# Order of the eight half rows at the seam between the spectral block and the feed-forward block

## The chip, the cores and the metric

The kernel runs on one NeuronCore of a Trainium2 chip, as one program. The metric is the device time of one execution in microseconds (us). Three executions of the kernel before took 1441.19, 1441.78 and 1444.77 us; the median, 1441.78 us, is the time that the changed kernel is compared with.

## What is computed

The input is one sequence of 4096 tokens with 640 channels. A conditioning vector gives six vectors of 640 values: shift, scale and gate for each of two blocks.

```python
h = _layernorm(x) * (1 + ca) + sa
x = x + ga * _A_ref(h, ...)      # 2-D real FFT, block-diagonal complex MLP with soft shrinkage, inverse FFT
h = _layernorm(x) * (1 + cb) + sb
x = x + gb * _B_ref(h, ...)      # (silu(h @ w_gate) * (h @ w_up)) @ w_down, inner width 1728
```

The two blocks are called the spectral block and the feed-forward block here. Everything is float32; matrix products are mostly done with numbers that are split in a high and a low part.

## The kernel before

**Tiling.** The 4096 tokens are seen as a grid of 128 (on the partitions) by 32 (n2). A "row" is one value of n2: 128 tokens by 640 channels. The spectral block goes through its frequencies in eight chunks, `ch` = 0 to 7, of four blocks each, so through 32 slots, p = 4·ch + b. A slot's last steps shrink the values (`shrink`), split them in two (`shrink_high` on ScalarE, `shrink_low` on VectorE: L847, `xl<-xx,xh`), and take the inverse transform over one axis (`stage_i`, L858 to L861: `pi`, then `co`). The result is stored to `s2` in DRAM. The feed-forward block needs rows of the finished inverse transform: a row loads its 128 frequencies from `s2`, multiplies them by a 128 by 128 matrix, gates the product with `gab`, adds the row of x, and normalizes it.

**The seam.** For the first four rows (tile 0 of the feed-forward block) this last part is written out by hand, and this is where the change lies. Each of these rows i = 0 to 3 is made in two halves: `hf` = 0 is the lower 320 columns, `hf` = 1 the upper 320. `cf` (tiles `cfrm` for rows 0 and 1, `cfrr` for rows 2 and 3) holds the frequencies loaded from `s2`. The last of these, 16 of 128, are stored and loaded again late, and for the lower columns only (`inverse_last(i, 0)`: L908 `pi<-tt,bx`, L909 `cz<-pi`, L910 store, then the load in L915). So there are two kinds of half row on TensorE:

- a lower half (L1086) is one product with the whole of `cf`, and waits for the late load;
- an upper half (L1089, L1091) takes the last chunk straight from `tt` in SBUF, four products with `et`, and one more with the first 112 rows of `cf`. It doesn't wait for the late load, and is five products where the lower half is one.

In the trace a product of two float32 operands counts as two matmuls.

**What follows each half row.** `first_y`: VectorE multiplies the sum in PSUM by `gab` (L1095, into one of four 320-column buffers in `acc` and `cl`); GpSimd adds it to x2 (L1096), VectorE for the last two half rows. `first_stats`: VectorE takes the statistics of the half (L1101); at the second half of a row it joins them (L1104, L1105), and GpSimd makes the scale and the shift from them in three small steps (L1106 power -0.5, L1108, L1109). `first_norm`: ScalarE normalizes rows 0, 1 and 2 into `xn` (L1115); row 3 is normalized by VectorE later (L2470). The loop that calls these goes through a list, `order`, of half rows in the order written by hand.

**What stands behind.** `inverse_last(i, 1)` does for the upper columns of the last chunk what was done for the lower ones: `pi` for i = 0 to 3 on TensorE (L908), into two PSUM banks taken in turn, `cz` on ScalarE (L909), and stores that GpSimd issues (L910). So the products of i = 2 and 3 wait until ScalarE has emptied the banks of i = 0 and 1. Then the feed-forward block begins: twenty transposes of `xn` on TensorE (L1923, `pt`, row by row and five to a row), the modulated result and its split (`ht`, `hx`: L1925, L1928, L1930, L1931), and the first gate products (`pg`, L1937 to L1939). The fifth transpose of each row goes to a bank that `inverse_last(3, 1)` has used.

**What sets the order.** Both parts stand under a manual schedule: each engine runs its instructions in an order fixed when the kernel is built, and waits for other engines by semaphores. In the feed-forward block a planner with a table of costs writes the order; it starts behind the seam and is not touched.

Of the kernel before, what the change touches and what calls it, by code (L numbers as in the profile page):

```python
# [9 lines left out]
OP = mybir.AluOpType  # L10
# [161 lines left out]
def body(tc, x, w1, b1, w2, b2, wg, wu, wd, c, wm, k_fa, k_tb, k_tx, k_bm, k_bx, k_ga, k_ge, k_id, out, dbg=None):  # L172
    nc = tc.nc
    pe, act, dve, pool = nc.tensor, nc.scalar, nc.vector, nc.gpsimd
# [27 lines left out]
    with ExitStack() as top:  # L202
# [34 lines left out]
        with ExitStack() as af:  # L237
# [351 lines left out]
            NP = 4 * NCH  # L589
# [274 lines left out]
            on = lambda f, p, *a: f(p // 4, p % 4, *a) if 0 <= p < NP else None  # L864
# [33 lines left out]
            def inverse_last(i, hf):  # L898
                e = slice(320 * hf, 320 * hf + 320)
                J = 4 * ORDER[NCH - 1] + i  # L900
                q, k = i // 2, slice(64 * (i % 2), 64 * (i % 2) + 64)
                if hf == 0:
                    xxs[NCH - 1, i] = p2.tile([P, D], F32, tag="xx", bufs=5, name=f"cz{i}")
                co = xxs[NCH - 1, i]
                pi = (ps.tile([P, 512], F32, tag="p3", name=f"pi{J}_{hf}") if hf == 0 else
                      bank0(i, [P, 512], f"pi{J}_{hf}"))
                for r in range(2):
                    mm(pi[:, :320], bx[k, r, :], tts[NCH - 1, q][k, r, e], start=(r == 0), stop=(r == 1))  # L908
                act.activation(co[:, e], pi[:, :320], AF.Copy)  # L909
                (pool if hf else nc.scalar).dma_start(s2[4 * J:4 * J + 4, :, e].rearrange("k n d -> (k n) d"), co[:, e])  # L910
# [109 lines left out]
            def first_gate():  # L1020
                src = wg.rearrange("(k p) f -> p k f", p=P)
                wraw.append(hp.tile([P, 4, 256], F32, tag="rz", bufs=2, name="wr4"))
                wraw.append(p2.tile([P, 256], F32, tag="wm", bufs=1, name="wr1"))
                nc.sync.dma_start(wraw[0], src[:, 0:4, 0:256])
                nc.sync.dma_start(wraw[1], src[:, 4, 0:256])

            def first_gate_high():
                for k in range(5):
                    act.activation(wh[k], wraw[0][:, k] if k < 4 else wraw[1], AF.Copy)
# [5 lines left out]
            def load_first():  # L1035
                x2 = fx.tile([P, 4, D], F32, tag="gx", bufs=2, name="x2_0")
                nc.sync.dma_start(x2, xv[:, 0:4, :])
                x2s[0] = x2
# [5 lines left out]
            for p in range(LAST + 1, NP):  # L1044
                if p > LAST + 1:
                    on(shrink, p - 5)
                on(stage_l1, p)
                on(tail_l1, p)
                if p == LAST + 1:
                    on(shrink, p - 5)  # L1050
                elif p == LAST + 2:
                    load_first()
                    first_gate()
                for f, *a in sums.get(p, ()):
                    f(*a)
                on(shrink_high, p - 5)
                on(stage_l2, p - 1)
                on(stage_i, p - 6)
                on(shrink_low, p - 5)
            first_gate_high()  # L1060
            on(shrink, LAST - 1)
            on(shrink_high, LAST - 1)
# [13 lines left out]
            x2 = x2s[0]  # L1076
            sts = lp.tile([P, 4, 2, 6], F32, tag="st", bufs=3, name="sts")

            def first_y(i, hf):
                e = slice(320 * hf, 320 * hf + 320)  # L1080
                g0 = et[:, i, 512:640]
                c = cf[i // 2][:, i % 2, e]
                tag = (("b0", "b1", "p1", "p1"), ("p2", "p2", "p3", "p3"))[hf][i]
                py = ps.tile([P, 512], F32, tag=tag, bufs=1 if tag[0] == "b" else 2, name=f"py0_{i}_{hf}")
                if hf == 0:
                    mm(py[:, :320], g0, c, start=True, stop=True)  # L1086
                else:
                    for k in range(4):
                        mm(py[:, :320], et[:, i, 128 * k:128 * k + 128], tts[NCH - 1, k // 2][:, k % 2, e],  # L1089
                           start=(k == 0), stop=False)  # L1090
                    mm(py[:, :320], g0[0:rl], c[0:rl], start=False, stop=True)  # L1091
                n = len(ys)
                y = (acc, cl)[n // 2 % 2][:, 320 * (n % 2):320 * (n % 2) + 320]
                ys.append(y)
                dve.tensor_tensor(y, py[:, :320], gab[:, e], op=OP.mult)  # L1095
                (pool if n < 6 else dve).tensor_tensor(x2[:, i, e], x2[:, i, e], y, op=OP.add)  # L1096


            def first_stats(i, hf):
                e = slice(320 * hf, 320 * hf + 320)  # L1100
                dve.bn_stats(sts[:, i, hf, :], x2[:, i, e])  # L1101
                if hf == i // 2:
                    mv, rs, nm = b1m[:, :, i], ca1[:, i:i + 1], sa4[:, i:i + 1]
                    dve.bn_aggr(mv, sts[:, i])  # L1104
                    dve.tensor_scalar(rs, mv[:, 1:2], EPS, None, op0=OP.add)  # L1105
                    pool.tensor_tensor(rs, rs, mhalf[:, :1], op=OP.pow)  # L1106
                    if i < 3:
                        pool.tensor_tensor(nm, mv[:, 0:1], rs, op=OP.mult)  # L1108
                        pool.tensor_tensor(nm, nm, mone[:, :1], op=OP.mult)  # L1109
                    fst.append((mv, rs, nm))  # L1110

            def first_norm(i):
                mv, rs, nm = fst[i]
                xn = p2.tile([P, D], F32, tag="co" if i < 2 else "wm", bufs=2 if i < 2 else 1, name=f"xn0_{i}")
                act.activation(xn, x2[:, i, :], AF.Identity, bias=nm, scale=rs)  # L1115
                xns[0].append(xn)

            ys = []
            fst = []
            order = [(0, 1), (1, 1), (0, 0), (1, 0), (2, 0), (3, 0), (2, 1), (3, 1)]  # L1120
            for n, (i, hf) in enumerate(order):
                first_y(i, hf)

                for q in ([n - 1] if 0 < n < 6 else [5, 6] if n == 6 else [7] if n == 7 else []):
                    first_stats(*order[q])
                if n in (3, 4):
                    first_norm(n - 3)
            for i in range(4):
                if i == 2:
                    first_norm(2)  # L1130
                inverse_last(i, 1)

        if dbg == "afno":
# [1428 lines left out]
```

## Time and profile before

| | |
|---|---|
| median of three executions | 1441.78 us |
| the profiled execution, its own time | 1442.52 us |
| its span, first to last instruction | 1440.7 us |
| TensorE busy | 1405.0 us, 98% |
| VectorE, ScalarE, GpSimd busy | 76%, 54%, 37% |
| stretch 280.00 to 321.07 us: TensorE busy | 35.98 of 41.07 us |
| the same: VectorE, ScalarE, GpSimd | 28.69, 19.76, 17.19 us |

The seam lies at about 285 to 321 us of the span. In the rows of the profile, PE is TensorE, PEld its weight loads, DVE VectorE, ACT ScalarE, POOL GpSimd and SP the engine that issues most transfers. A row of the timeline has the start, the duration (of several instructions, from the first start to the last end), the engine and line, what is written and read, and the count; in square brackets the time that the engine sat idle before it, and who ended that.

### The profile page before, as it was taken

The numbers are of one execution on the slowest core, as the hardware profiler recorded it, in microseconds if no ns is written. First come the engines' busy times: TensorE is split into PE (matmuls) and PEld (weight loads), VectorE is DVE, ScalarE is ACT, GpSimd is POOL, SyncE is SP. The second block draws the span as 40 slices with busy tenths as digits, with TensorE's granted clock in tenths as the row PEclk, the third lists the DMA queues.
The fourth block names the chain that finished last, engine by engine and source line by source line (L and its number), as shares of the span: only waits on it lengthen the run. The fifth ranks groups of instructions, "written<-read, shape, count | busy, mean of one in ns | idle before, by whom it ended". The sixth has DMA issues, their size and how long they took to land.

```text
span 1440.7 us, 23922 instructions
## 1 busy us (share of the span) xinstructions
PE 1405.0 (98%) x8516; PEld 1329.6 (92%) x8516; DVE 1100.3 (76%) x1979; ACT 783.8 (54%) x1560; POOL 538.6 (37%) x640
## 2 busy tenths in 40 slices
PE   7899999989999999999999999999999999999999
PEld 2699999968889888899999999999999999999998
DVE  8878888868888687767878778788647757567775
ACT  6868877745544545545465556555435345245432
POOL 5300222144444444333244334434324545146533
PEclk9999999999999999999999999999999999999999
DMA  9988798757777989897787997788896666966652
GB/s 375 319 267 261 238 293 257 226 175 248 251 243 256 349 267 303 309 359 259 252 306 237 344 370 242 252 275 284 291 330 225 209 219 237 361 218 226 207 184 91
DMA packets 187383, 382.28 MB, mean 265 GB/s; under 512 B 22240, under 2 KB 104736, under 8 KB 185472
## 3 DMA queue, kind: packets, MB, share of 16 engines
q1 hardware_dynamic: 179072, 364.37, 73.7%
q0 software_dynamic: 6608, 13.77, 3.0%
q10 hardware_dynamic: 1584, 2.62, 0.5%
q8 instruction: 67, 1.10, 0.3%
q14 instruction: 52, 0.43, 0.1%
HBM read 266.66 MB, written 104.86 MB: 258 GB/s over the span
## 4 chain that ended last, share of the span: by engine, by line
PE 80%; DVE 8%; DMA 5%; ACT 3%; issue 2%; SPq 1%; POOL 1%; DVEq 0%; ACTq 0%; POOLq 0%
PE pd L2432 15%; PE pw L2113 8%; PE pw L2115 8%; PE pw L2114 8%; PE pd_X L2294 5%; PE pg L1978 3%; PE pg L1977 3%; PE pg L1979 3%; PE pc L800 3%; PE pl L732 3%; PE pd_Y L2294 3%; PE pw L2124 2%; PE pw L2126 2%; PE pw L2125 2%; PE py L1699 1%
## 5 line engine op out<-in xcount | busy, mean ns | idle before, releaser
L2432 PE MATMUL pd<-wdh,a 128*128 128x320 f32 x1040 | 240.1, 311 | 1.1 <-DVE x L2404 1.1
L2432 PEld LDWEIGHTS pd<-wdh,a 128*128 128x128 f32 x1040 | 177.2, 189 | 1.7 <-DVE x L2404 1.4
L2432 PE MATMUL pd<-wdl,a 128*128 128x320 f32 x540 | 166.7, 310 | 0.0
L1454 DVE TENSOR_TENSOR wb<-r,wb 128x512 fp32r<-128x512 f32 (+3 forms) x154 | 154.7, 1015 | 12.1 <-ACT wb L1451 10.5
L2113 PE MATMUL pw<-h,wt 128*128 128x384 f32 x416 | 141.2, 340 | 2.2 <-ACT s_x L2132 2.2
L2115 PE MATMUL pw<-h,wt 128*128 128x384 f32 x416 | 140.3, 337 | 0.0
L2114 PE MATMUL pw<-h,wt 128*128 128x384 f32 x416 | 139.9, 336 | 0.0
L2404 DVE TENSOR_TENSOR x<-x,pd 128x320 f32<-128x320 f32 x240 | 109.8, 479 | 37.9 <-PE pd L2432 33.6
L1451 ACT ACTIVATE wb<-r 128x512 fp32r<-128x512 f32 (+3 forms) x170 | 117.4, 704 | 35.5 <-PE pw L2126 24.5
L2113 PE MATMUL pw<-h,wb 128*128 128x384 f32 x312 | 105.0, 336 | 0.9 <-DVE x L2404 0.9
L2114 PE MATMUL pw<-h,wb 128*128 128x384 f32 x312 | 104.6, 335 | 0.0
L2115 PE MATMUL pw<-h,wb 128*128 128x384 f32 x312 | 104.6, 335 | 0.0
L1977 PE MATMUL pg<-ht,wb 128*128 128x512 f32 x260 | 102.3, 393 | 0.0
L2432 PEld LDWEIGHTS pd<-wdl,a 128*128 128x128 f32 x540 | 101.9, 189 | 0.3
L1979 PE MATMUL pg<-ht,wb 128*128 128x512 f32 x260 | 101.4, 390 | 0.2 <-DVE wb L1454 0.2
L1978 PE MATMUL pg<-ht,wb 128*128 128x512 f32 x260 | 101.5, 390 | 0.0
L2132 ACT ACTIVATE s_x<-pw 128x384 f32<-128x384 f32 x52 | 25.5, 490 | 121.3 <-PE pw L2115 120.2
L1682 POOL TENSOR_TENSOR cr<-cr,gab 128x640 f32<-128x640 f32 x28 | 46.7, 1670 | 94.1 <-DMA cr<-s 75.9
L2113 PEld LDWEIGHTS pw<-h,wt 128*128 128x128 f32 x416 | 78.1, 188 | 3.8 <-ACT s_x L2132 3.8
L862 POOL DMA_DIRECT2D s<-co x28 | 15.9, 569 | 167.3 <-ACT co L861 158.4
L2114 PEld LDWEIGHTS pw<-h,wt 128*128 128x128 f32 x416 | 78.2, 188 | 0.0
L2115 PEld LDWEIGHTS pw<-h,wt 128*128 128x128 f32 x416 | 78.1, 188 | 0.0
(360 smaller groups left out, 4060.2 us busy)
## 6 DMA issues: line engine op xcount, KB each, us to landing
wt<-td SPq DMA_DIRECT2D x104, 512.0 KB, 5.1
hs<-ho SPq DMA_DIRECT2D x52, 512.0 KB, 5.4
h<-hs SPq DMA_DIRECT2D x32, 768.0 KB, 8.4
r<-in_B_w_up_dram SPq DMA_DIRECT2D x36, 640.0 KB, 5.0
r<-in_B_w_gate_dram SPq DMA_DIRECT2D x36, 640.0 KB, 4.8
wdr<-wdd SPq DMA_DIRECT2D x25, 640.0 KB, 5.9
td<-wt SPq DMA_DIRECT2D x25, 512.0 KB, 5.8
g<-s SPq DMA_DIRECT2D x7, 1280.0 KB, 8.7
```

Of the source, the lines that this page charges most:

```text
L1451: act.activation(wbs[t, n][:, 0, ks, e], raw[t, n][:, ks, e], AF.Copy)
L1454: (pool if onp else dve).tensor_tensor(wbs[t, n][:, 1, ks, e], raw[t, n][:, ks, e], f32(wbs[t, n][:, 0, ks, e]), op=OP.subtract)
L1682: pool.tensor_tensor(crs[r], crs[r], gab, op=OP.mult)
L1977: mm(b, wh, hh, start=(kk == 0), stop=False)
L1978: mm(b, wh, hl, start=False, stop=False)
L1979: mm(b, wl, hh, start=False, stop=(kk == 4))
L2113: mm(b, w(0, kp), a[:, kp, 0], start=start and kp == 0, stop=False, skip_group_check=not start)
L2114: mm(b, w(0, kp), a[:, kp, 1], start=False, stop=False, skip_group_check=not start)
L2115: mm(b, w(1, kp), a[:, kp, 0], start=False, stop=kp == 1, skip_group_check=not start)
L2294: mm(bk[b, i][:, :320], x, y, start=new and j == 0, stop=j == len(seq) - 1, skip_group_check=not new)
L2404: dve.tensor_tensor(x2[:, e], x2[:, e], x[0][:, :320], op=OP.add)
L2432: mm(pd[g, hf][0][:, :320], l, m, start=i == 0, stop=i == len(s) - 1 and not (last and len(gs) > 1))
```

## The change

Three edits, all at the seam:

1. In the last slot (p = 31) `shrink_low` of slot 26 stands ahead of `stage_l2` and `stage_i` instead of behind them, so VectorE makes `xl` ahead of the two additions to `tt`.
2. The half rows come in the order upper 0, 1, 2, then lower 0, 1, 2, then upper 3, lower 3 (before: upper 0, 1, lower 0, 1, 2, 3, upper 2, 3). All rows are complete with their lower half. GpSimd adds seven of the eight half rows instead of six.
3. The three calls of `first_norm` follow half rows 4, 5 and 6 of the list, so all stand ahead of `inverse_last(i, 1)`; before, the third stood between i = 1 and i = 2 of it.

```diff
                 on(shrink_high, p - 5)
+                if p == NP - 1:
+                    on(shrink_low, p - 5)
                 on(stage_l2, p - 1)
                 on(stage_i, p - 6)
-                on(shrink_low, p - 5)
+                if p < NP - 1:
+                    on(shrink_low, p - 5)
...
-                (pool if n < 6 else dve).tensor_tensor(x2[:, i, e], x2[:, i, e], y, op=OP.add)
+                (pool if n < 7 else dve).tensor_tensor(x2[:, i, e], x2[:, i, e], y, op=OP.add)
...
-                if hf == i // 2:
+                if hf == 0:
...
-            order = [(0, 1), (1, 1), (0, 0), (1, 0), (2, 0), (3, 0), (2, 1), (3, 1)]
+            order = [(0, 1), (1, 1), (2, 1), (0, 0), (1, 0), (2, 0), (3, 1), (3, 0)]
             for n, (i, hf) in enumerate(order):
                 first_y(i, hf)
 
-                for q in ([n - 1] if 0 < n < 6 else [5, 6] if n == 6 else [7] if n == 7 else []):
+                for q in ([n - 1] if 0 < n < 7 else [6, 7] if n else []):
                     first_stats(*order[q])
-                if n in (3, 4):
-                    first_norm(n - 3)
+                if n in (4, 5, 6):
+                    first_norm(n - 4)
             for i in range(4):
-                if i == 2:
-                    first_norm(2)
                 inverse_last(i, 1)
```

On TensorE, the half rows of the seam; `py_i_hf` is the PSUM sum of row i, half hf. Before:

```order
L1091 MATMUL py_1_1_3899<-cfrm,et 128x320
L1086 MATMUL py_0_0_3908<-cfrm,et 128x320
L1086 MATMUL py_1_0_3913<-cfrm,et 128x320
L1086 MATMUL py_2_0_3925<-cfrr,et 128x320
L1086 MATMUL py_3_0_3937<-cfrr,et 128x320
L1089 MATMUL py_2_1_3942<-tt_0_3595,et 128x320 x2
L1089 MATMUL py_2_1_3942<-tt_1_3606,et 128x320 x2
L1091 MATMUL py_2_1_3942<-cfrr,et 128x320
L1089 MATMUL py_3_1_3957<-tt_0_3595,et 128x320 x2
L1089 MATMUL py_3_1_3957<-tt_1_3606,et 128x320 x2
L1091 MATMUL py_3_1_3957<-cfrr,et 128x320
L908 MATMUL pi_1_3969<-tt_0_3595,bx 128x320 x2
```

The same place on TensorE with the change (the line numbers are those of the changed file, three higher):

```order
L1094 MATMUL py_1_1_3899<-cfrm,et 128x320
L1092 MATMUL py_2_1_3908<-tt_0_3595,et 128x320 x2
L1092 MATMUL py_2_1_3908<-tt_1_3606,et 128x320 x2
L1094 MATMUL py_2_1_3908<-cfrr,et 128x320
L1089 MATMUL py_0_0_3917<-cfrm,et 128x320
L1089 MATMUL py_1_0_3922<-cfrm,et 128x320
L1089 MATMUL py_2_0_3934<-cfrr,et 128x320
L1092 MATMUL py_3_1_3946<-tt_0_3595,et 128x320 x2
L1092 MATMUL py_3_1_3946<-tt_1_3606,et 128x320 x2
L1094 MATMUL py_3_1_3946<-cfrr,et 128x320
L1089 MATMUL py_3_0_3962<-cfrr,et 128x320
L908 MATMUL pi_1_3971<-tt_0_3595,bx 128x320 x2
```

The upper half of row 2 has moved ahead of the first lower half, and the lower half of row 3 to the end; the number of products is the same.

On ScalarE, from the normalization of row 0 to the first `ht`; `xn_i` are the normalized rows, the four `cz` the evacuations of `inverse_last(i, 1)`, i = 0 to 3 in this order. Before:

```order
L1115 ACTIVATE xn_0_3923<-x_0_3673,sa_72,ca_71 128x640
L1115 ACTIVATE xn_1_3935<-x_0_3673,sa_72,ca_71 128x640
L909 ACTIVATE cz_3859<-pi_1_3969 128x320
L909 ACTIVATE cz_3865<-pi_1_3974 128x320
L1115 ACTIVATE xn_2_3979<-x_0_3673,sa_72,ca_71 128x640
L909 ACTIVATE cz_3871<-pi_1_3981 128x320
L909 ACTIVATE cz_3877<-pi_1_3986 128x320
L1925 ACTIVATE ht_3_4009<-pt_0_4035,sb_74,cb_73 128x512
```

The same place on ScalarE with the change:

```order
L1118 ACTIVATE xn_0_3932<-x_0_3673,sa_72,ca_71 128x640
L1118 ACTIVATE xn_1_3944<-x_0_3673,sa_72,ca_71 128x640
L1118 ACTIVATE xn_2_3960<-x_0_3673,sa_72,ca_71 128x640
L909 ACTIVATE cz_3859<-pi_1_3971 128x320
L909 ACTIVATE cz_3865<-pi_1_3976 128x320
L909 ACTIVATE cz_3871<-pi_1_3981 128x320
L909 ACTIVATE cz_3877<-pi_1_3986 128x320
L1926 ACTIVATE ht_3_4009<-pt_0_4035,sb_74,cb_73 128x512
```

The normalization of row 2 has moved ahead of the first two `cz`.

On GpSimd, from the fifth addition to x2 to the first store of `cz`; `ca` and `sa` are the scale and the shift of a row, in three steps to a row. With the change:

```order
L1099 TENSOR_TENSOR x_0_3673<-x_0_3673,acc 128x320
L1109 TENSOR_TENSOR ca_71<-ca_71,mhalf 128x1
L1111 TENSOR_TENSOR sa_72<-b1m,ca_71 128x1
L1112 TENSOR_TENSOR sa_72<-sa_72,mone 128x1
L1099 TENSOR_TENSOR x_0_3673<-x_0_3673,acc 128x320
L1109 TENSOR_TENSOR ca_71<-ca_71,mhalf 128x1
L1111 TENSOR_TENSOR sa_72<-b1m,ca_71 128x1
L1112 TENSOR_TENSOR sa_72<-sa_72,mone 128x1
L1099 TENSOR_TENSOR x_0_3673<-x_0_3673,cl 128x320
L1109 TENSOR_TENSOR ca_71<-ca_71,mhalf 128x1
L1111 TENSOR_TENSOR sa_72<-b1m,ca_71 128x1
L1112 TENSOR_TENSOR sa_72<-sa_72,mone 128x1
```

Ahead of the three steps of row 2 stand seven additions and the steps of rows 0 and 1; before, there were six additions and the same steps, with one addition fewer ahead of each of the three.

Two more moves need no rows. On TensorE the first two transposes of row 0 stand ahead of the last two `pi` of `inverse_last(i, 1)`; before, all twenty stood behind them. On VectorE the first edit is one move: L847 `xl_2<-xx_2,xh_2` now stands directly behind L774 and ahead of the two L802 `tt<-pc,b2t`, where before it stood behind both.

## Prediction

> **What bounds the kernel now.** First the busy time by stretch. The columns behind the bounds are the length and then the busy us (and count) of PE, PEld, DVE, ACT and POOL.
>
> ```profile
> 280.00:321.07 41.07, 35.98 (x183) 26.70 (x181) 28.69 (x61) 19.76 (x41) 17.19 (x29) 1.00 0.47 153
> 321.07:1440.70 1119.63, 1108.05 (x6554) 1070.12 (x6554) 840.26 (x1449) 548.09 (x1086) 458.16 (x495) 1.00 0.77 265
> ```
>
> Behind the seam TensorE is busy for 1108.05 of 1119.63 us. What remains open there is 11.6 us, and the largest entry of its waits is on another engine's work, not on a transfer:
>
> ```profile
> PE pw L2124 <- ACT s_z L2132: 2.5, 2, 1.9
> ```
>
> Such a wait moves with the work before it. So I carry a shift of the seam's end to the end of the program one to one. Ahead of that, the 41.07 us of the seam have 5.1 us in which TensorE does nothing, and there order can matter. I read the seam on each engine in order of time. First PE:
>
> ```profile
> 298.67 2.32 PE L1089 MATMUL py<-tt,et 128*128 128x320 f32 x8
> 300.82 0.70 PE L1091 MATMUL py<-cfrm,et 112*128 112x320 f32 x2
> 303.27 1.34 PE L1086 MATMUL py<-cfrm,et 128*128 128x320 f32 x4 [1.74 <-DMA cfrm<-s]
> 305.53 2.32 PE L1089 MATMUL py<-tt,et 128*128 128x320 f32 x8
> 307.68 0.70 PE L1091 MATMUL py<-cfrr,et 112*128 112x320 f32 x2
> 310.38 0.70 PE L1091 MATMUL py<-cfrr,et 112*128 112x320 f32 x2
> 311.01 1.35 PE L908 MATMUL pi<-tt,bx 64*128 64x320 f32 x8
> 312.88 1.67 PE L908 MATMUL pi<-tt,bx 64*128 64x320 f32 x8 [0.51 <-ACT cz L909]
> 314.48 2.56 PE L1923 MATMUL pt<-idn,xn 128*128 128x128 f32 x20
> ```
>
> TensorE stands still for 1.74 us until the late load lands (303.27), then runs through to 312.36, waits 0.51 us for `cz`, and makes the transposes. Eight products of an upper half take 307.68 - 305.53 = 2.15 us, so 0.27 each: 2.69 us an upper half, 0.54 a lower half. Now ACT:
>
> ```profile
> 307.74 0.92 ACT L1115 ACTIVATE xn<-x,sa,ca 128x640 f32<-128x640 f32 x1 [11.44 <-POOL sa L1109]
> 312.39 0.77 ACT L909 ACTIVATE cz<-pi 128x320 f32<-128x320 f32 x2 [1.86 <-PE pi L908]
> 313.32 0.92 ACT L1115 ACTIVATE xn<-x,sa,ca 128x640 f32<-128x640 f32 x1 [0.17 <-POOL sa L1109]
> 314.25 0.77 ACT L909 ACTIVATE cz<-pi 128x320 f32<-128x320 f32 x2
> 316.64 0.78 ACT L1925 ACTIVATE ht<-pt,sb,cb 128x512 fp32r<-128x512 f32 x1 [1.62 <-PE pt L1923]
> ```
>
> The first `cz` begins at 312.39, as soon as TensorE delivers. From there everything to the first `ht` (316.64) follows: `pi` of i = 2 and 3 at +0.49, the bank for the fifth transpose free at +2.63 (314.25 + 0.77), `ht` at +4.25. **The seam's end is the first `cz` plus 4.25 us**, as long as `xn` of rows 2 and 3 is there.
>
> **The order of the half rows.** The upper half of row 2 needs nothing late, so it fills the wait. The half row at 298.67 and its L1091 at 300.82 end their issue at 301.36, and row 2's upper half runs from 301.36 to 304.06, past the landing at 303.27. Then three lower halves to 305.68, row 3 upper to 308.38, row 3 lower to 308.92. Before, L1091 at 310.38 issued until 310.92. So TensorE finishes the half rows **2.0 us earlier**, and `pi` of i = 0 and 1 end at 310.36 instead of 312.36. This alone would bring `cz` to 310.39.
>
> **But `cz` no longer waits for TensorE.** On ScalarE it now stands behind `xn` of row 2, and that needs the statistics of row 2, so the additions and the three steps on GpSimd. Their prices, DVE first, then POOL:
>
> ```profile
> 301.57 0.49 DVE L1095 TENSOR_TENSOR acc<-py,gab 128x320 f32<-128x320 f32 x1 [2.20 <-PE py L1091]
> 304.52 0.48 DVE L1101 BATCH_NORM_STATS2 sts<-x 128x6 f32<-128x320 f32 x1
> 304.92 0.47 DVE L1095 TENSOR_TENSOR cl<-py,gab 128x320 f32<-128x320 f32 x1
> 305.58 0.50 DVE L1101 BATCH_NORM_STATS2 sts<-x 128x6 f32<-128x320 f32 x1 [0.18 <-POOL x L1096]
> 306.11 0.21 DVE L1104 BATCH_NORM_AGGREGATE b1m<-sts 128x2 f32<-128x12 f32 x1
> 306.36 0.15 DVE L1105 TENSOR_SCALAR ca<-b1m 128x1 f32<-128x1 f32 x1
> 306.43 0.48 DVE L1095 TENSOR_TENSOR acc<-py,gab 128x320 f32<-128x320 f32 x1
> 306.82 0.48 DVE L1101 BATCH_NORM_STATS2 sts<-x 128x6 f32<-128x320 f32 x1
> ```
>
> ```profile
> 304.68 1.68 POOL L1096 TENSOR_TENSOR x<-x,cl 128x320 f32<-128x320 f32 x2 [1.69 <-DVE cl L1095]
> 306.59 0.58 POOL L1106 TENSOR_TENSOR ca<-ca,mhalf 128x1 f32<-128x1 f32 x1 [0.22 <-DVE ca L1105]
> 307.65 0.87 POOL L1096 TENSOR_TENSOR x<-x,acc 128x320 f32<-128x320 f32 x1
> ```
>
> An addition takes 0.84 us in a pair and 0.86 otherwise. The three steps take 307.65 - 306.59 = 1.06 us until the next addition, and ScalarE's `xn` starts 307.74 - 306.59 = 1.15 after the first of them. VectorE starts 0.05 after a sum is complete (301.52 to 301.57), GpSimd 0.08 after VectorE. From statistics to the end of L1105 is 306.51 - 305.58 = 0.93, to GpSimd 1.01.
>
> So with the change: row 2's upper sum is complete at 304.22, L1095 at 304.27, its addition 304.84 to 305.68. VectorE then waits for that addition with the statistics (305.74), makes L1095 of row 1 lower 0.40 later (306.14, done 306.61), whose addition, the fifth, runs 306.69 to 307.55. Meanwhile the fourth (305.68 to 306.52) completes row 0: statistics at 306.58, L1105 done and handed over at 307.59. From here GpSimd alone sets the pace: three steps 1.06, sixth addition 0.86, three steps 1.06, seventh addition 0.86, that is 3.84 us to 311.43, and then 1.15: `xn` of row 2 at 312.58 (before: 313.32). It holds ScalarE for 0.93 (313.32 to 314.25), so **the first `cz` begins at 313.51 instead of 312.39: +1.1 us**. The two transposes now ahead of `pi` save nothing, since the fifth waits for the last `cz` as before. Row 3 isn't late: its last addition stays on VectorE, its scale comes a little over 1 us after that of row 2, and its transposes follow fifteen others behind the last `cz`.
>
> **The move of `shrink_low`.** DVE, ACT and PE where it stands:
>
> ```profile
> 285.81 0.89 DVE L802 TENSOR_TENSOR tt<-pc,b2t 128x320 f32<-128x320 f32 x2
> 286.61 0.82 DVE L847 TENSOR_TENSOR xl<-xx,xh 128x640 fp32r<-128x640 f32 x1
> ```
>
> ```profile
> 285.23 0.72 ACT L842 ACTIVATE xh<-xx 128x640 fp32r<-128x640 f32 x1
> ```
>
> ```profile
> 287.48 0.42 PE L859 MATMUL pi<-xl,bm 128*128 128x320 f32 x1 [1.07 <-DVE xl L847]
> ```
>
> `xl` can start once `xh` is there, at about 285.98, so 0.63 us earlier, and L859 follows. But VectorE, which began the additions at 285.81, now starts with `xl` 0.17 later, and so comes all behind it: `xx` and `xl` of slot 27, for which the next L859 waits, and the shrinking of `tt`, which `inverse_last` and the upper halves need. The gain of 0.63 on TensorE is given back there. I book 0, with 0.2 either way.
>
> **The sum** is +1.1 us: 1442.52 + 1.1 = 1443.6 for the profiled execution, which was 0.74 above the median; on the median **1442.9**. The bounds, beside the 0.2: the seventh addition on GpSimd may meet the eighth on VectorE. Before, two such met, DVE first, then POOL:
>
> ```profile
> 309.48 0.49 DVE L1096 TENSOR_TENSOR x<-x,cl 128x320 f32<-128x320 f32 x1
> ```
>
> ```profile
> 309.53 1.17 POOL L1096 TENSOR_TENSOR x<-x,acc 128x320 f32<-128x320 f32 x1
> ```
>
> It cost GpSimd 0.31 us. By my times GpSimd starts first now (310.57; VectorE comes to its addition 1.35 after the statistics of row 2 at 309.57, so at 310.92), and I take 0; the other end is +0.31. In the stretch behind the seam such meetings shift too; a few of them could give or take up to about 1 us. That makes +0.0 to +2.4 for this case: 1441.8 to 1444.2.
>
> **The rivals.** *The earlier half rows reach the end.* If GpSimd were through 1.1 us sooner, the loss would be gone; if `cz` began when TensorE delivers, at 310.39, `ht` would come 2.0 earlier: 1439.8. For it speaks that TensorE is the engine of the critical chain; against it, that ScalarE runs in order and that the seven additions and nine steps leave GpSimd hardly a pause from 304.84 on. Chance 0.1.
>
> *The delay is swallowed.* GpSimd's stores of `cz` and the loads of rows behind them hardly move; where a later wait hangs on these, the 1.1 us vanish: 1441.8, within 0.6. Against it: the 11.6 us of open time behind the seam are mostly waits on engines. Chance 0.22.
>
> *TensorE's clock falls.* With the change TensorE has nothing but two transposes from 310.36 until `pi` of i = 2 at 314.0, some 3.3 to 3.6 us. After the long idle time at the program's start its products ran at half pace for a while (weight loads of equal products):
>
> ```profile
> 8.07 0.50 PEld L421 LDWEIGHTS pa<-xa,fa 128*128 128x128 f32 x2 [8.07 <-ACT xa L401]
> 12.50 0.34 PEld L421 LDWEIGHTS pa<-xa,fa 128*128 128x128 f32 x1 [0.52 <-ACT xa L401]
> 13.36 0.34 PEld L421 LDWEIGHTS pa<-xa,fa 128*128 128x128 f32 x1 [0.52 <-issue]
> 14.92 0.19 PEld L421 LDWEIGHTS pa<-xa,fa 128*128 128x128 f32 x1 [0.24 <-issue]
> 15.35 0.19 PEld L421 LDWEIGHTS pa<-xa,fa 128*128 128x128 f32 x1 [0.24 <-issue]
> ```
>
> The spacing is 0.86 us up to 13.4 and 0.43 from 14.9, though the granted clock reads 1.00 throughout. The 1.74 us before 303.27 did no such harm (four products in 1.34). If 3.5 us do, the second `pi` group (1.67) and the transposes (2.56) take up to twice as long: at most +4.2, on top of the 1.1. Part of both spans is waiting, so I take +3.1: 1446.0. It decides from an idle time somewhere between 1.74 and 8.07 us. Chance 0.08. [...]
>
> **How the numbers follow.** The forecast has 0.6. Forecast and the swallowed delay hold 0.82 and span 1441.2 to 1444.2; with some room for the spread of the three runs (1441.19 to 1444.77) I give 1440.9 to 1444.6. About 0.3%, 4.3 us, is what a measurement of this kernel can tell from no change. All cases but the clock's lie within it: faster 0.02, within 0.95, slower 0.03.
>
> **What would show it.** Right: no wait at L1086, `pi` of i = 0 and 1 done near 310.4, then ScalarE's `xn` of row 2 near 312.6 waiting for GpSimd, `cz` behind it, TensorE idle for over 3 us, the first `ht` near 317.7. Wrong: `cz` before 312.4; weight loads of the transposes at twice their spacing; or a first `ht` that is late by 1 us in a run that isn't.

## The result and the profile after

The changed kernel took 1446.59 us (median of 8 runs, 1441.83 to 1451.96), the kernel before, run beside it, 1441.93 us (8 runs, 1439.5 to 1444.89): a ratio of 1.0037, 95% interval 1.0024 to 1.0050. That is 3.5 to 7.2 us slower, most likely 5.3; the prediction had 1442.9 and a range up to 1444.6. The profiled execution took 1447.18 us, its span is 1445.4 us.

First the seam on TensorE in the trace after:

```profile
303.29 2.32 PE L1092 MATMUL py<-tt,et 128*128 128x320 f32 x8
305.44 0.70 PE L1094 MATMUL py<-cfrr,et 112*128 112x320 f32 x2
305.99 1.24 PE L1089 MATMUL py<-cfrm,et 128*128 128x320 f32 x4
...
310.93 1.35 PE L908 MATMUL pi<-tt,bx 64*128 64x320 f32 x8
312.21 0.44 PE L1924 MATMUL pt<-idn,xn 128*128 128x128 f32 x2
315.90 2.82 PE L908 MATMUL pi<-tt,bx 64*128 64x320 f32 x8 [3.24 <-ACT cz L909]
318.65 2.57 PE L1924 MATMUL pt<-idn,xn 128*128 128x128 f32 x18
321.65 0.51 PE L1938 MATMUL pg<-ht,wh 128*128 128x512 f32 x1 [0.43 <-ACT ht L1926]
321.99 0.40 PE L1939 MATMUL pg<-ht,wl 128*128 128x512 f32 x1
324.53 0.50 PE L1940 MATMUL pg<-ht,wh 128*128 128x512 f32 x1 [2.14 <-DVE ht L1932]
```

The wait at the late load is gone (no bracket at 305.99). In its place stand two others: 3.24 us ahead of the second `pi` group and 2.14 us ahead of the first product with the lower half of `ht`. The second `pi` group takes 2.82 us instead of 1.67. ScalarE in the same trace:

```profile
314.60 0.92 ACT L1118 ACTIVATE xn<-x,sa,ca 128x640 f32<-128x640 f32 x1 [1.18 <-POOL sa L1112]
315.43 0.74 ACT L909 ACTIVATE cz<-pi 128x320 f32<-128x320 f32 x2
318.43 0.77 ACT L909 ACTIVATE cz<-pi 128x320 f32<-128x320 f32 x2 [2.26 <-PE pi L908]
320.82 0.78 ACT L1926 ACTIVATE ht<-pt,sb,cb 128x512 fp32r<-128x512 f32 x1 [1.62 <-PE pt L1924]
```

`xn` of row 2 waits for GpSimd and holds up the first `cz`, as predicted. But from the first `cz` to the first `ht` it is 5.39 us instead of 4.25. Each `ht` is split in a high part, which ScalarE makes, and a low part, which VectorE makes by a subtraction; the texts below call the low part the lower half of `ht`, and it has nothing to do with the half rows. VectorE, then GpSimd, where TensorE waits 2.14 us for the first of these:

```profile
322.30 2.17 DVE L1932 TENSOR_TENSOR ht<-hx,ht 128x512 fp32r<-128x512 f32 x1 [6.17 <-ACT hx L1929]
```

```profile
319.27 1.14 POOL L910 DMA_DIRECT2D s<-cz  x2 [1.88 <-ACT cz L909]
...
322.51 0.73 POOL L1499 TENSOR_TENSOR ts<-r 128x256 f32<-128x256 f32 x1
323.19 0.72 POOL L1499 TENSOR_TENSOR ts<-r,ts 128x256 f32<-128x256 f32 x1
```

The subtraction that makes the first lower half takes 2.17 us (0.92 before) and ends behind the two subtractions `ts` of GpSimd (differences of blocks of the weights), which are late because GpSimd issues the late stores of `cz` first. Last, busy time and granted clock by stretch; the columns behind the bounds are length, busy us of PE, PEld, DVE, ACT, POOL, then the clock (1.00 is full), the DMA share and GB/s:

```profile
310.93:315.90 4.97, 1.73 (x12) 0.91 (x11) 3.72 (x11) 2.84 (x5) 3.87 (x9) 0.99 0.01 3
315.90:319.25 3.35, 3.35 (x10) 2.18 (x11) 0.23 (x1) 1.04 (x3) 1.14 (x2) 0.50 0.28 98
319.25:322.66 3.41, 2.71 (x19) 2.03 (x18) 0.36 (x1) 1.84 (x3) 3.21 (x6) 1.00 0.28 99
322.66:326.08 3.42, 1.55 (x7) 1.28 (x8) 3.42 (x4) 3.42 (x6) 1.65 (x3) 1.00 0.81 236
326.08:329.49 3.41, 3.41 (x10) 2.63 (x9) 3.34 (x5) 1.45 (x3) 1.72 (x2) 0.50 0.76 224
```

Twice TensorE runs at clock 0.50, each time for one stretch of 3.41 us (called a window from here on; 315.84 to 319.25 and 326.08 to 329.49 in the trace's record of the clock), and each time the stretch of the same length ahead of it was largely idle: 0.23 and 1.55 us of work in 3.41. The kernel before has one such window in its trace, far behind the seam, with the same sign ahead of it (a wait of 1.89 us from 687.7 to 689.6):

```profile
686.30:689.70 3.40, 1.51 (x10) 1.19 (x9) 3.40 (x7) 0.90 (x2) 0.07 (x1) 1.00 0.47 162
689.70:693.10 3.40, 3.40 (x13) 3.40 (x14) 2.96 (x8) 2.67 (x7) 0.00 (x0) 0.51 0.97 338
```

### The profile page after: what moved, and what is told of

Its sections match the earlier page's. It is cut to its first block, busy times and chain, and to the rows that moved or that the text cites. A ratio compares the mean times of both kernels' runs of the same rounds, so it can differ in the third digit from the quotient of the medians.

```text
span 1445.4 us, 23923 instructions
## 1 busy us (share of the span) xinstructions
PE 1405.4 (97%) x8516; PEld 1330.0 (92%) x8516; DVE 1100.7 (76%) x1978; ACT 784.2 (54%) x1560; POOL 537.1 (37%) x641
## 4 chain that ended last, share of the span: by engine, by line
PE 72%; DVE 10%; DMA 8%; ACT 5%; issue 2%; POOL 2%; SPq 1%; DVEq 0%; ACTq 0%; POOLq 0%
PE pd L2433 14%; PE pw L2114 8%; PE pw L2116 8%; PE pw L2115 8%; PE pd_X L2295 5%; PE pg L1979 3%; PE pg L1978 3%; PE pg L1980 3%; PE pd_Y L2295 2%; PE pw L2125 2%; PE pc L800 2%; PE pw L2127 2%; PE pw L2126 2%; PE pl L732 2%; DVE wb L1455 2%
```

## The experiments

**Theory A**, formed on these traces: the loss is the order on ScalarE (+1.1 us) and what the gap that it opens does to TensorE's clock. **Rival B**: the loss sits in GpSimd's later work behind the seam, and the clock is only a sign. Later **theory C** (the lateness of the order alone) and **D** (the trace of before was a long one) came in. Ratios are to the kernel before, run on the same chip, with 95% intervals; 0.001 is 1.44 us. Single executions scatter by about 2 us (standard deviation 1.8 to 2.4 us over the 21 to 35 executions of the kernel before in a set), so every kernel is also read at three points of its trace, at the end of this section.

**e1_between, e2_behind: only ScalarE's order undone.** The half rows, GpSimd's seventh addition and the move of `shrink_low` stay. In e1 `xn` of row 2 stands between the second and the third `cz`, as before; in e2 behind the fourth (`first_norm(2)` after the loop).

```diff
-                if n in (4, 5, 6):
+                if n in (4, 5):
                     first_norm(n - 4)
             for i in range(4):
+                if i == 2:
+                    first_norm(2)
                 inverse_last(i, 1)
```

> The change without its third edit: the normalization of row 2 stands again between the second and the third cz. Theory A (ScalarE's order opens a gap on TensorE, and TensorE's clock falls in it): the first two cz begin when TensorE delivers, 2 us earlier than before, the gap of over 3 us is gone, no half-clock stretch in it, and the first ht comes 0.5 to 1 us earlier than before relative to the half rows: time -1.5 to +0.5 against before. Rival B (the loss sits in GpSimd's later work and the collisions behind the seam, the clock being only a sign of it): most of the +4.7 stays, +2 to +5.

> The change, but the normalization of row 2 stands behind all four cz. Theory A: all cz go as TensorE delivers, the fifth transpose waits for nothing, the sixteenth is bound by rows 2 and 3 being normalized near 314 us: first ht 1.5 to 2 us earlier than before, no half clock in the seam: -2.5 to 0 against before, and under e1. Rival B: +2 to +5.

Measured: 0.9995 (0.9982 to 1.0008) and 0.9993 (0.9981 to 1.0006); neither trace has a half-clock window ahead of the program's last microseconds (mean granted clock 1.000 in both, where one window takes off 0.0012). TensorE in e1, with 1.50 us where the change has 3.24:

```profile
307.02 1.35 PE L908 MATMUL pi<-tt,bx 64*128 64x320 f32 x8
309.87 1.67 PE L908 MATMUL pi<-tt,bx 64*128 64x320 f32 x8 [1.50 <-ACT cz L909]
```

So without the third edit's order on ScalarE the loss is gone: the rest of the change alone costs nothing that can be measured. (A had e2 below e1; the two can't be told apart.)

**e3_fill: the gap filled.** The full change; TensorE multiplies a constant tile 14 times while it would wait, into a bank that nobody reads.

```diff
             for i in range(4):
+                if i == 2:
+                    pz = ps.tile([P, P], F32, tag="p1", name="pz2")
+                    for _ in range(14):
+                        mm(pz, ones, ones, start=True, stop=True)
                 inverse_last(i, 1)
```

> The full change, with 14 products of a constant tile (some 3 us of work, read by nobody) put on TensorE between the second and the third pi, so into the gap. Nothing else moves: ScalarE's order and the late cz stay. Theory A: the clock stays at 1.00 through the seam's pi and transposes, the first ht keeps only the +1.1 of ScalarE's order, and the time falls from +4.7 to between +1 and +3 against before. Rival B: the filler changes nothing, +4 to +5.5.

Measured: 1.0036 (1.0025 to 1.0047), as slow as the change. TensorE, and then the windows:

```profile
311.19 3.39 PE L1135 MATMUL pz<-ones 128*128 128x128 f32 x28
314.86 1.67 PE L908 MATMUL pi<-tt,bx 64*128 64x320 f32 x8 [0.28 <-ACT cz L909]
...
322.33 0.50 PE L1944 MATMUL pg<-ht,wh 128*128 128x512 f32 x1 [2.15 <-DVE ht L1936]
```

```profile
320.20:323.70 3.50, 1.36 (x6) 1.14 (x7) 3.50 (x4) 3.50 (x6) 1.54 (x4) 1.00 0.70 180
323.70:327.10 3.40, 3.40 (x10) 2.62 (x9) 3.33 (x4) 1.63 (x3) 2.06 (x2) 0.50 0.88 279
```

The first half-clock window is gone (`pi` again in 1.67), so the gap had caused it. But the blocked lower half and the second window stay, and the time didn't fall: it came as B said, and A was at best incomplete.

**e4_early: ScalarE's order alone**, on the kernel before.

```diff
+            first_norm(2)
             for i in range(4):
-                if i == 2:
-                    first_norm(2)
                 inverse_last(i, 1)
```

> Before, with the third edit's order on ScalarE alone: all three normalizations ahead of the four cz, half rows in the old order. The first cz then waits for the normalization of row 2 (313.32 + 0.93 = 314.25 instead of 312.39). Theory A: +1.9 from the order, TensorE's gap is 2.4 us, and where a clock window falls on it badly 1 to 3 us more: +1.5 to +4.5. Rival B: +1.9 at most, since the half rows and GpSimd's work are those of before: 0 to +1.9.

Measured: 1.0009 (0.9997 to 1.0021), which is 1.3 us (-0.4 to 3.0), as B said. In the trace, the slowest of the twelve executions, a gap of 2.24 us was enough for a half-clock window: the second `pi` group takes 2.15 us, the first seventeen transposes 3.22. The first lower half takes 0.93 us here. So the order on ScalarE is needed for the loss, but on the old half rows it loses less than the full change does.

```profile
313.31 1.35 PE L908 MATMUL pi<-tt,bx 64*128 64x320 f32 x8
316.90 2.15 PE L908 MATMUL pi<-tt,bx 64*128 64x320 f32 x8 [2.24 <-ACT cz L909]
318.98 3.22 PE L1922 MATMUL pt<-idn,xn 128*128 128x128 f32 x17
```

**e5_sp, e6_sp_fill, e8_sp_before: the stores on SyncE.** The four late stores are issued by SyncE, so that GpSimd's subtractions come earlier: in the full change (e5), in e3 (e6) and in the kernel before (e8).

```diff
-                (pool if hf else nc.scalar).dma_start(s2[4 * J:4 * J + 4, :, e] ...
+                (nc.sync if hf else nc.scalar).dma_start(s2[4 * J:4 * J + 4, :, e] ...
```

> The full change, but the stores of the upper halves of cz are issued by SyncE instead of GpSimd, so that GpSimd's subtractions ts come some 5 us earlier, ahead of the lower halves ht on VectorE. Theory A now has three parts: the order on ScalarE (+1.1), TensorE at half clock in a window that the gap opens (+1.2), and the first lower half of ht held up beside GpSimd's ts (2.17 us instead of about 0.9, +0.8) with a second half-clock window behind that wait (+1.4). A: the first lower half takes 0.7 to 0.95 us, the second window is gone, the first may stay: the seam's shift is +1.1 to +2.4 instead of +4.4, and the time against before +1 to +3 us (ratio 1.0007 to 1.002). Rival B: the loss is the lateness itself and moving GpSimd's work gives nothing: first lower half short, but the shift stays over +3.5 and the ratio at 1.003 or more.

> As the one before, and 14 products of ones on TensorE in the gap ahead of pi of i = 2 (they write a tile that nobody reads). A: neither half-clock window is left, the first lower half is short, and only the order on ScalarE remains: seam shift +0.9 to +1.4, time against before +0.5 to +1.5 us (ratio 1.0003 to 1.001). B: ratio 1.003 or more as with the filler alone (1.0036).

> The kernel before with only the stores of the upper halves of cz issued by SyncE instead of GpSimd: what that move is worth by itself. Before, GpSimd's ts run at 316.95 to 320.46 beside the first three lower halves of ht (0.92, and 2.16 for two); with them 2.3 us earlier these should take 0.7 to 0.9 each. A: the seam ends 0.3 to 0.8 us earlier, time within 1 us of before (0.9994 to 1.0003). B: the stores on SyncE hold up its loads, the time rises by 1 us or more.

Measured: 1.0061 (1.0049 to 1.0073), 1.0051 (1.0035 to 1.0066), 1.0022 (1.0012 to 1.0032). The lower halves take 0.69 us and the second window is gone, yet all three are slower than the kernel before: this edit has a cost of its own. SyncE's queue in e8:

```profile
310.09 2.80 SPq L910 DMA_DIRECT2D s<-cz  x4
312.99 0.39 SPq L1433 DMA_DIRECT2D r<-in_B_w_up_dram  x1
```

SyncE waits for `cz` with the stores, and the weight loads queued behind them come at 312.99 instead of 302.37. GpSimd's subtractions wait for these loads, so they come later and not earlier (the first at 321.16 in e8, at 316.95 before) and miss the lower halves on the other side. TensorE then waits 3.10 us at 352.07 (1.14 before). From the 30th product of the table below to the end these three take 1118.9 to 1119.6 us, some 5 us more than the others, so they settle nothing on the time of the seam.

**e7_fill2: both gaps filled.** As e3, and 7 products of the constant behind the first two products on `ht`; the stores are GpSimd's again.

```diff
                         mm(pg[f], w1, ht0[k][:, 0, :], start=False, stop=False)
+                        if k == 0 and f == 0:
+                            for _ in range(7):
+                                mm(pz, ones, ones, start=True, stop=True)
                         mm(pg[f], w0, ht0[k][:, 1, :], start=False, stop=(k == 4))
```

> The full change with the 14 products of ones in the gap and 7 more behind the first two products on ht, where TensorE waits for the first lower half; GpSimd's stores stay where the change has them. It parts the second half-clock window from the wait ahead of it. A: the first lower half still takes over 2 us and TensorE's products on ht still start that much late, but at full clock (0.23 us apart throughout): seam shift +1.8 to +2.2, 1.2 to 1.4 less than with the first filler alone (+3.2), time against before +1.5 to +3. Rival B: the clock was only a sign, and the shift stays at +3.2.

Measured: 1.0020 (1.0009 to 1.0030). The lower half still takes 2.18 us, but no half-clock window falls in the seam or right behind it:

```profile
320.00:323.50 3.50, 2.47 (x18) 2.13 (x18) 2.35 (x2) 3.50 (x6) 2.67 (x5) 1.00 0.50 147
323.50:327.00 3.50, 3.50 (x16) 2.83 (x17) 3.47 (x5) 2.88 (x5) 2.11 (x2) 1.00 0.87 272
```

Against e3 the last of the 30 products on `ht` comes 1.5 us earlier, and the time is 2.3 us less, though the intervals just overlap: the second window is a cost of its own, and idle time brings it.

**e9_act, e10_act_fill, e11_act_before, e12_between_act: the stores on ScalarE**, behind the last `cz`, where it waits for transposes; SyncE's order stays. In the full change (e9), in e3 (e10), in the kernel before (e11), in e1 (e12).

```diff
-                (pool if hf else nc.scalar).dma_start(s2[4 * J:4 * J + 4, :, e] ..., co[:, e])
+                late.append((s2[4 * J:4 * J + 4, :, e] ..., co[:, e]))
+                if hf == 0 or i == 3:
+                    for a in late:
+                        nc.scalar.dma_start(*a)
+                    late.clear()
```

> The full change, with the four stores of cz issued by ScalarE behind the last cz (4 times 0.34 us, in the 1.6 us in which it waits for the transposes) instead of by GpSimd. SyncE's queue keeps its order, which the run with the stores on SyncE did not: there five weight loads stood behind the stores. GpSimd's ts then start near the last pow, some 4 us earlier. Theory A: the first lower half of ht takes 0.7 to 0.95 us instead of 2.17, no half-clock window behind it; the first window may stay. Seam shift +1.1 to +2.4 us, time against before +1 to +3 (ratio 1.0007 to 1.002). Rival C (the lateness of the order alone makes the loss): ratio 1.003 or more as with the full change.

> As the one before, with the 14 products of ones in the gap ahead of pi of i = 2: no half-clock window in the seam and no blocked lower half, only the order on ScalarE. Theory A: seam shift +0.9 to +1.4 in the profile, time against before +0.3 to +1.5 us (ratio 1.0002 to 1.001). Rival C: +4 us or more (1.003).

> The kernel before with the four stores of cz issued by ScalarE behind the last cz: the control. A: the first three lower halves of ht take 0.69 each instead of 0.92 and 1.08, the seam ends 0 to 0.4 us earlier, time within 1 us of before. C says the same.

> The order with xn of row 2 between the second and third cz (first two edits of the change kept) and the stores on ScalarE: a candidate for a version faster than before. A: the seam ends 1.2 to 1.8 us earlier than before's and no gap reaches 2 us, time 1 to 2 us under before (ratio 0.9987 to 0.9995). C: ratio within 0.0005 of 1.

Measured: 1.0015 (1.0002 to 1.0027), 1.0022 (1.0011 to 1.0033), 0.9993 (0.9979 to 1.0006), 0.9993 (0.9983 to 1.0003). In e9 the lower half takes 0.69 us (VectorE, then GpSimd):

```profile
322.70 0.69 DVE L1938 TENSOR_TENSOR ht<-hx,ht 128x512 fp32r<-128x512 f32 x1 [6.35 <-ACT hx L1935]
```

```profile
321.47 0.72 POOL L1505 TENSOR_TENSOR ts<-r,ts 128x256 f32<-128x256 f32 x1
```

With GpSimd done before VectorE begins, the change loses 2.2 us (0.3 to 3.9) instead of 5.3 (3.5 to 7.2): e9 came as A said. e10, with nothing left but the order, should have lost 0.3 to 1.5 and lost 1.6 to 4.8, so neither A nor C has its number. The mean times of e9 and e10 lie 2.5 and 3.2 us above that of their control e11. So the order costs more than the 1.1 us of the two traces; and filling the gap, which is all that parts e10 from e9, gained no time (0.8 us slower, interval -0.6 to 2.2). And e11's trace, like e8's, had no 1.74 us wait at the late load, though nothing ahead of it was changed.

**e13_before, e14_before, e15_before, e16_after: further traces** of the two kernels, unchanged. (Where the recorded texts say the first upper `cz` of the last slot, from which they count, the first `cz` of its lower halves is meant.)

> The kernel before again, for another trace. In the traces so far SyncE issues the load of the last rows either about 4 us or about 6 us after the load ahead of it, and TensorE's 1.74 us wait stands in the late ones alone. Theory D: both happen in the kernel before; with the late load the first ht starts 23.5 us after the first upper cz of the last slot, with the early one 22.0 to 22.5; the change (24.5 with its gap filled) then costs 1.0 against the one and 2.0 to 2.5 against the other. Rival: the wait of 1.74 is always there in this kernel, and the early load came with the moved stores.

> The kernel before, a further trace, as the one ahead of it. D: of the traces of this very kernel some have the early load, with the first ht at 22.0 to 22.5. Rival: all at 23.4 to 23.6.

> The kernel before, a third further trace, as the two ahead of it. D: of the traces of this very kernel some have the early load, with the first ht at 22.0 to 22.5. Rival: all at 23.4 to 23.6.

> The changed kernel again, for a second trace. D and A: whether the load is early or late, TensorE doesn't wait for it, the first upper cz to the first lower cz of row pair 0 stays 20.2 to 20.6 us, and the half-clock window in the gap of 3.2 us strikes again (first ht at 25.6 to 25.9; 24.5 without); the first lower half of ht again takes about 2.2 us. Rival: the windows were chance, none in this trace.

SyncE's loads of the first rows in the trace that the prediction used, then in e14:

```profile
295.33 0.32 SPq L915 DMA_DIRECT2D cfrm<-s  x1
295.70 0.41 SPq L915 DMA_DIRECT2D cfrr<-s  x1
301.48 0.32 SPq L915 DMA_DIRECT2D cfrm<-s  x1
```

```profile
295.54 0.32 SPq L915 DMA_DIRECT2D cfrm<-s  x1
295.92 0.42 SPq L915 DMA_DIRECT2D cfrr<-s  x1
299.35 0.32 SPq L915 DMA_DIRECT2D cfrm<-s  x1
```

TensorE and ScalarE in e14:

```profile
301.76 1.24 PE L1086 MATMUL py<-cfrm,et 128*128 128x320 f32 x4
```

```profile
310.78 0.77 ACT L909 ACTIVATE cz<-pi 128x320 f32<-128x320 f32 x2 [1.59 <-PE pi L908]
```

The load is issued 6.15 us behind the first in one trace, 3.81 in the other, and with the early one TensorE doesn't wait. Of the four traces of the kernel before two are late (6.15, 6.19) and two early (3.81, 4.24): D holds, though e15 (first `ht` at 22.83) lies outside what D gave. What makes it late is in the trace's record of the landings. SyncE issues the load 0.13 to 0.14 us after the last of the sixteen parts of the last store has landed, in all twenty traces of this document. In the late trace shown fifteen parts are down by 299.22 and the sixteenth at 301.34, in e13 by 300.06 and at 302.27, in e17, below, by 300.14 and at 302.21; in e14 all are down at 299.21. Why one part comes some 2 us behind the others in some executions no run shows.

In e16 the gap is again 3.26 us and again followed by a window of half clock (granted clock 0.61 on average from 312.83 to 317.10), which now covers part of `pi` and part of the transposes:

```profile
312.83 2.29 PE L908 MATMUL pi<-tt,bx 64*128 64x320 f32 x8 [3.26 <-ACT cz L909]
315.05 3.27 PE L1924 MATMUL pt<-idn,xn 128*128 128x128 f32 x18
...
320.67 0.51 PE L1940 MATMUL pg<-ht,wh 128*128 128x512 f32 x1 [1.18 <-DVE ht L1932]
```

The first lower half did not take 2.2 us again, as was expected, but 1.20: with the transposes at half clock, VectorE comes to it later, beside the last `ts` alone (it starts 0.78 us behind the start of the third `ts`, where it started 0.21 ahead of it in after). TensorE waits 1.18 us for it, and there is no second half-clock window. In all twelve traces in which it takes over 0.75 us (the four of before, after, e2, e3, e4, e7, e16, e17, e18) the first lower half ends 0.55 to 0.56 us after the end of a `ts`, and in the other eight it takes 0.69 to 0.75 us (0.69 in e8 and e9, with no `ts` beside it). So by these traces it waits for GpSimd, and how long depends on where the two fall.

**e17_low, e18_order: the change in two parts.** e17 has only the move of `shrink_low`, e18 all but this.

> The move of shrink_low alone, on the kernel before. By the traces it gains about 0.9 us on the first product on xl and gives it back on the next two: 0, time within 1 us of before (0.9993 to 1.0007). If it carries a part of the loss that the order does not explain: ratio 1.001 or more.

> The change without the move of shrink_low: only the order of the half rows and of ScalarE. It should carry all of the loss: ratio 1.0025 to 1.0045, a gap of about 3.2 us on TensorE with a window of half clock in or behind it, the first ht 25.4 to 26.0 us behind the first upper cz of the last slot, and the first lower half of ht beside GpSimd's ts. If the move of shrink_low matters: under 1.002.

Measured: 1.0005 (0.9992 to 1.0018) and 1.0029 (1.0015 to 1.0043). The half rows and ScalarE's order carry the loss. e18 has the gap (3.25 us) and the window (eighteen transposes in 3.63 us); its first lower half takes 0.86 us, TensorE waits 0.83 us for it, and no second window follows.

**All traces at three points**, in us from the first `cz` of the lower halves of the last slot (293.13 in the first trace): first upper `cz`, first `ht`, and the last of the 30 products on the first `ht` tiles, each a difference of two starts.

| kernel (traces) | first upper cz | first ht | 30th product |
|---|---|---|---|
| before, late load (2) | 19.26, 19.30 | 23.51, 23.56 | 32.94, 33.52 |
| before, early load (2) | 17.91, 18.44 | 22.31, 22.83 | 32.58, 33.00 |
| order on ScalarE undone: e1, e2 | 18.13, 18.70 | 22.59, 23.08 | 31.81, 33.09 |
| change, gap open: after, e16, e18 | 20.53, 20.43, 20.41 | 25.92, 26.00, 25.97 | 37.57, 35.57, 35.21 |
| gap open, GpSimd's stores moved: e5, e9 | 20.26, 20.25 | 25.65, 25.82 | 34.32, 35.03 |
| gap filled: e3, e7 | 20.24, 20.25 | 24.47, 24.48 | 36.11, 34.60 |
| gap filled, stores moved: e6, e10 | 20.26, 20.25 | 24.49, 24.48 | 33.16, 34.17 |
| stores moved alone, early load: e8, e11 | 17.67, 18.07 | 22.06, 22.46 | 30.72, 31.14 |
| e4, e12, e17 | 20.98, 18.75, 18.98 | 26.68, 23.21, 23.24 | 35.92, 33.28, 33.38 |

From the 30th product to the end it is 1111.7 to 1114.7 us in the four traces of before, 1112.9, 1114.8 and 1113.5 in after, e16 and e18.

## Why the prediction was wrong

*The half rows end 2.0 us earlier*: right against the trace used; `pi` of i = 0 and 1 start 16.03 us behind the first lower `cz` (294.90 in after) instead of 17.88, so 1.85 earlier.

*The first `cz` comes 1.1 us later*: right in mechanism, too small in size. ScalarE waits for GpSimd's chain, and the first upper `cz` stands at 20.2 to 20.5 in every trace of that order, whatever the load does. What it is compared with was mis-sized: 19.26 is the late form. Before, `cz` follows TensorE, and with the early load comes at 17.9 to 18.4. The order's cost at the first `ht` is 24.48 less 23.53, so 0.95, against the late form and 1.65 to 2.2 against the early one. The prediction took the wait of 1.74 us as a property of the kernel; one trace can't show whether it is one. At the 30th product the early form has lost most of its lead (33.00, 32.58 against 32.94, 33.52). By the times the term is larger still: e10, with no half-clock window in the seam and no blocked lower half, loses 1.6 to 4.8 us. Where these come from no trace shows.

*"The seam's end is the first `cz` plus 4.25 us"*: the step that failed on TensorE. It is 4.23 with the gap filled and 5.4 to 5.6 with it open, in all five traces with the gap of 3.2 us (after, e5, e9, e16, e18). The rival "TensorE's clock falls" named this and had a chance of 0.08, its author's estimate: in the trace of before no wait of TensorE lies between 1.89 us and the 8.07 us at the program's start, so what a gap of 3.5 us does could not be read there. In the runs, after a window with 1.55 (after), 1.51 (before) or 1.36 us (e3) of work in about 3.4, the next one ran at half clock.

In each of the twenty traces all half-clock windows, up to its last microseconds, lie on one grid of 3.41 us (in after they begin at 315.84 and 326.08, so 10.24 apart, three times 3.413). Counted along it, all 21 windows with at most 1.55 us of work on TensorE were followed by half clock (in after 0.23 and 1.55 us, in before 1.52), and none of the 14 with 1.59 to 1.65 us was (in after 1.59 from 29.12 on). (Of those with 1.65 to 2.64 us eleven were, all in the spectral block; why, no run shows.) All twenty traces have the wait of 1.89 to 1.95 us near 690 us, and a half-clock window follows it in nine of them: in before it lies within one window, which has 1.52 us of work, and half clock follows; in after it lies across two, with 2.61 and 2.32 us of work, and none follows. Half clock followed the gap of 3.2 us in five of five, and the late load's wait of 1.58 to 1.77 us in none of four (before, e13, e4, e17). So in these traces somewhat over half a window idle (1.87 of 3.41 us in after) was enough. Estimated from the 3.41 and the 1.9 us, a wait of 1.9 us would strike when it lies within one window of the grid, which is (3.41 - 1.9) / 3.41 = 0.44 of all positions, and one of 3.2 us nearly wherever the grid lies.

The price was +3.1 in the rival and is 1.2 to 1.5 at the first `ht`, since a window holds 3.4 us and part of the work in it was waiting anyway. That the rival's 1446.0 lies so near the measured 1446.59 is luck: its price is over twice what the traces show, and the collisions make up for it.

In the times not even this price is seen: with the gap filled the loss stayed at 1.0036 against 1.0037 (e3 against the change) and at 1.0022 against 1.0015 (e10 against e9). For e3 the traces offer a reason: with the gap filled, as in after, the first lower half starts 0.21 us ahead of GpSimd's third `ts` and takes 2.18 us (e3, e7), against 1.20 and 0.86 with the gap open (e16, e18). For e10, where nothing is blocked, they offer none; its interval leaves room for a gain of 0.6 us at most.

*Collisions behind the seam, booked at 0 with up to about 1 us*: the other step that failed. GpSimd's stores moved with `cz`, its subtractions with them, and met VectorE's first lower half. That is 1.25 us on VectorE against the trace of before and, in after and e3, 2.14 us of waiting on TensorE (0.90 before), which brought the second half-clock window. From the first `ht` to the 30th product it is 11.6 us in these two, 9.2 and 9.6 in e18 and e16, 9.4 to 10.3 in before, 8.7 in e5 and e6: before pays for such a meeting too. In the times this term is the one that shows: without the collision the loss is 2.2 us instead of 5.3 (e9), without the second window 2.9 instead of 5.2 (e7 against e3).

*The move of `shrink_low` is worth 0*: right (e17). *The shift is carried one to one*: not contradicted, but the rest of the program scatters by 3 us from trace to trace (the last sentence of the table), so 1 or 2 us more or less would not show.

Two smaller points. The half pace at the program's start, which the prediction noted at a granted clock of 1.00, is no riddle: in before the trace's record of the clock begins at 13.9 us, and the last slow row is at 13.36. And the bounds of the sum (0.2 either way, up to 0.31 and 1 either way) give -0.1 to +2.6 and not +0.0 to +2.4, which changes nothing here.

**The sum.** At the 30th product the three traces of the change's order stand at 36.1 on average, the four of before at 33.0: 3.1 us, of which 1.4 are the order, 1.5 the window in the gap and 0.2 the rest. The timed loss is 3.5 to 7.2 us, in e18 2.2 to 6.2. The traces and the times don't divide the loss alike: by the times the order takes about 3 us, the collision and the second window 2 to 3, the first window nothing that can be told from 0. The traces of e16 and e18 are of quick executions (1444.07 and 1443.99 us, where the medians are 1446.59 and 1445.86), and neither has the second window, so part of the difference may lie in how often that strikes. The rest stays open.

None of e1, e2, e11 and e12 is measurably faster than the kernel before: all four stand at 0.9993 to 0.9995, each with 1 in its interval.

## What to carry to other kernels

Before one takes a wait as the thing to be removed, one should see it in several traces of the unchanged kernel: this one was there in two of four. A step that needs a long chain of other engines can cost little behind work that is ready, and much ahead of it: here `xn` of row 2 behind two or four `cz` left the ratio at 0.9995 and 0.9993 (e1, e2), and ahead of them it is 1.0037. A gap on TensorE should be looked at for a window at half clock behind it: the gap of 3.2 us brought one in five of five traces and cost 1.2 to 1.5 us at the next stage, though the time of the whole program did not show it; a wait of 1.9 us brought one in nine of twenty. And work that a change makes later on one engine should be followed to the next engine that it meets: here that cost 2 to 3 us by the times, more than the window.

## What was not expected of the hardware

- In these traces half clock came in windows of 3.41 us, behind windows that were idle for 3.18 and 1.87 us (after) or 1.89 us (before), so also in the kernel before, and in eleven cases for less; the same wait of 1.9 us was followed by one in before and not in after, which may be part of the scatter of single times.
- A VectorE subtraction of two SBUF tiles that the trace starts 0.21 us ahead of GpSimd's (322.30 and 322.51) still ended behind GpSimd's second (2.17 us instead of 0.69).
- The load behind a store was issued either about 4 or about 6 us after the load ahead of it, in otherwise equal traces of one kernel: in the late ones a single part of sixteen of the last store landed 2.1 to 2.2 us behind the rest, and SyncE issued the load 0.13 to 0.14 us after the last of the sixteen.
